# Second feature pair of the first chunk by seven block products, with its loads re-ordered, in a GeGLU kernel

## The chip, the cores and the metric

One NeuronCore of a Trainium2 chip. The metric is the device time of one execution in microseconds (us), shorter is better. Each kernel's runs were timed beside runs of the kernel before on the same chip. A **ratio** below is the mean time of one kernel's fast runs over the mean of the other's of the same rounds, so it is not quite the ratio of the medians that stand beside it; the square brackets hold its 95% interval.

## The reference, cut to what matters

```python
B, S, D, F = 1, 2048, 1024, 3584          # bf16 x [S, D], w_gate and w_up [D, F], w_down [F, D]
def reference(x, w_gate, w_up, w_down):
    return (gelu_tanh(x @ w_gate) * (x @ w_up)) @ w_down
```

## The kernel before

Tokens go in two halves of 1024, each two **token blocks** of 512. A **feature block** is 128 columns of the weights, a **pair** two of them, a **chunk** four (512 columns). D is eight slices of 128, called kd 0 to 7. A **slot** is one TensorE matmul of a 128x128 weight block with a 512 wide moving operand. One pair on two token blocks with both matrices is 2 x 2 x 2 x 8 = 64 slots when multiplied directly. From the second chunk on, every pair is done by Strassen's scheme in Winograd's form: seven products M1 to M7 of blocks of half of D instead of eight, 7 x 2 x 4 = 56 slots. M1 and M2 take the bf16 data as they lie; the five others take sums of weight blocks ("left sums", s1 to s4 and a22) and of x blocks ("right sums", t1 to t4 and b22) in the 32-bit type fp32r, which VectorE, GpSimd and ScalarE have to make first. A **bank** is one of the tiles that TensorE writes its results to. The very first chunk of the kernel is done directly, because there is nobody yet to have made sums. Its start:

```python
    load_x0(0, sp)                              # first 256 columns of x, token block 0
    load_w(first, 0, 0, 2, act, 0, FA)          # gate, kd 0-1, first 256 of 512 columns
    load_w(first, 1, 0, 2, sp, 0, FA)           # up
    load_x0(1, act)
    load_w(first, 0, 2, 5, act, 0, FA)
    load_w(first, 1, 2, 5, sp, 0, FA)
    # ... act table, identity, NWARM = 8 matmuls on constants ...
    for kd in range(KH, KD):                    # KH = 4, KD = 8
        load_xT(xT, 0, 0, kd, kd + 1)           # transposing loads of x, SyncE's queue
        if kd == KH + 1:
            for j in range(2):
                load_w(first, j, 5, KD, act, 0, FA)
    for j in range(2):
        load_w(first, j, 0, KD, sp, FA, FG)     # the other 256 columns, all kd
    for k0 in range(0, KD, KH):
        load_xT(xT, 0, 1, k0, k0 + KH)          # token block 1
    new_chunk((0, 1))
    for j in range(2):
        load_w((0, 1), j, 0, KD)
```

and its computation, ahead of the loop over the pairs:

```python
    def first_units(hT):                        # feature blocks 0 and 1, token block 0
        transpose_x0(0)                         # first x by TensorE transposes
        for kd, j in [(kd, j) for kd in range(KD) for j in range(2)]:
            for u in range(2):
                mm_gu(banks[held[u][j]], (wg, wu)[j], u, 0, kd)
            if (j, kd) == (1, 0):
                transpose_x0(1)
        # ...
            first_units(hT)
            unit(hT, PB, 2, 0)                  # unit(bank set, feature block, token block)
            t_sum("t1")
            unit(hT, QB, 3, 0)
            t_sum("t2")
            t_sum("b22")
            unit(hT, VB, 0, 1)
            t_sum("t3")
            for name in S_NAMES:                # left sums of the next chunk's first pair
                for j in range(2):
                    s_sum(0, PPG, j, name)      # on GpSimd
            unit(hT, RB, 1, 1)
            t_sum("t4")
            unit(hT, QB, 2, 1)
            unit(hT, VB, 3, 1)
```

## Time and profile before

| | before |
|---|---|
| time, median of 4 runs | 541.57 us (541.2 to 542.12) |
| instructions | 7102, of them 2392 matmuls and transposes |
| first pair of the second chunk starts at | 33.80 us |
| next pair after it | 12.56 us later |
| granted TensorE clock | full in every slice |

Two rows say what the first chunk is. The first line below is the page's header; the second is a group (line, engine, operation, shapes, count; then busy us and mean ns of one; then TensorE's idle time just ahead of them). The last two are the stretch 17 to 20 us in the windows view (busy us and number of instructions of TensorE, its weight loads, VectorE, ScalarE, GpSimd; granted clock; DMA share; GB/s).

```profile
span 539.7 us, 7102 instructions
```
```profile
L252 PE MATMUL bank<-xT,w_mem 128*128 128x512 bf16 x128 | 28.4, 379 | 0.3 <-DVE xT L310 0.2
```
```profile
core 0: us, PE busy (x) PEld busy (x) DVE busy (x) ACT busy (x) POOL busy (x), PEclk, DMA share, GB/s
...
17.00:20.00 3.00, 3.00 (x16) 1.35 (x15) 2.69 (x2) 1.54 (x4) 0.00 (x0) 1.00 1.07 291
```

The reader is to see that 128 direct slots stand in 28.4 us with 0.3 us of idle time ahead of all of them. There is nothing to win here but slots; the mark to watch is the start of the next chunk's first pair, 33.80 us, since everything behind it is the same program in both kernels.

### The profile page before, as it was taken

The numbers are of one execution on the slowest core, as the hardware profiler recorded it, in microseconds if no ns is written. First come the engines' busy times: TensorE is split into PE (matmuls) and PEld (weight loads), VectorE is DVE, ScalarE is ACT, GpSimd is POOL, SyncE is SP. The second block draws the span as 40 slices with busy tenths as digits, with TensorE's granted clock in tenths as the row PEclk, the third lists the DMA queues.
The fourth block names the chain that finished last, engine by engine and source line by source line (L and its number), as shares of the span: only waits on it lengthen the run. The fifth ranks groups of instructions, "written<-read, shape, count | busy, mean of one in ns | idle before, by whom it ended". The sixth has DMA issues, their size and how long they took to land.

```text
span 539.7 us, 7102 instructions
## 1 busy us (share of the span) xinstructions
PE 535.1 (99%) x2392; PEld 374.5 (69%) x2392; DVE 354.9 (66%) x466; ACT 258.9 (48%) x438; POOL 235.0 (44%) x206
## 2 busy tenths in 40 slices
PE   9999999999999999999999999999999999999997
PEld 3457777666776676767776677777777766866865
DVE  1767777787775997889574434444444469969951
ACT  2435555555555319216465555555555551452270
POOL 0197777777776000000056776666777730000000
PEclk9999999999999999999999999999999999999999
DMA  9928577696827876779950405041331466677946
GB/s 233 310 82 230 185 242 237 184 286 195 277 76 252 299 244 227 249 265 313 327 182 1 155 2 156 7 149 57 99 106 51 157 204 213 226 241 246 291 145 207
DMA packets 84771, 102.70 MB, mean 190 GB/s; under 512 B 18688, under 2 KB 66304, under 8 KB 84736
## 3 DMA queue, kind: packets, MB, share of 16 engines
q1 hardware_dynamic: 61936, 80.30, 46.2%
q10 hardware_dynamic: 22800, 21.96, 13.2%
q8 instruction: 19, 0.31, 0.2%
q14 instruction: 16, 0.13, 0.1%
HBM read 85.98 MB, written 12.58 MB: 183 GB/s over the span
## 4 chain that ended last, share of the span: by engine, by line
PE 98%; DMA 1%; ACTq 0%; ACT 0%; issue 0%
PE bank L386 61%; PE bank L656 33%; PE bank L252 5%; DMA w_mem<-in_w_gate_dram 1%; ACTq L161 0%; ACT xT L312 0%; ACT o_sb L709 0%; ACTq L167 0%; ACTq L709 0%
## 5 line engine op out<-in xcount | busy, mean ns | idle before, releaser
L386 PE MATMUL bank<-t_mem,s_mem 128*128 128x512 f32 x1016 | 239.8, 394 | 0.0
L386 PEld LDWEIGHTS bank<-t_mem,s_mem 128*128 128x128 f32 x1016 | 190.8, 188 | 41.9
L358 POOL TENSOR_TENSOR s_mem<-w_mem 128x512 fp32r<-128x512 bf16 x100 | 115.8, 1178 | 201.3 <-DMA w_mem<-in_w_up_dram 104.6
L276 DVE TENSOR_TENSOR hT<-w_mem,bank 128x512 bf16<-128x512 f32 x104 | 71.3, 686 | 92.4 <-PE bank L386 46.3
L656 PE MATMUL bank<-t_mem,s_mem 128*128 128x512 f32 x544 | 127.2, 392 | 0.0
L656 PEld LDWEIGHTS bank<-t_mem,s_mem 128*128 128x128 f32 x544 | 102.1, 188 | 22.2 <-issue 0.2
L409 DVE TENSOR_TENSOR bank<-bank,m 128x512 f32<-128x512 f32 x104 | 67.3, 694 | 46.9 <-ACT m L431 45.3
L386 PE MATMUL bank<-xT,w_mem 128*128 128x512 bf16 x416 | 94.3, 380 | 0.0
L271 ACT ACTIVATE w_mem<-bank 128x512 f32<-128x512 f32 x104 | 61.9, 596 | 57.7 <-DVE bank L409 32.7
L386 PEld LDWEIGHTS <-w_mem 128*128 128x128 bf16 x416 | 38.7, 98 | 49.7 <-issue 6.5
L566 DVE TENSOR_TENSOR t_mem<-w_mem 128x1024 fp32r<-128x1024 bf16 x56 | 65.5, 1216 | 0.0
L358 POOL TENSOR_TENSOR s_mem<-w_mem,s_mem 128x512 fp32r<-128x512 bf16 x50 | 62.1, 1267 | 0.0
L358 POOL TENSOR_TENSOR s_mem<-s_mem,w_mem 128x512 fp32r<-128x512 f32 x50 | 59.6, 1212 | 0.0
L371 ACT CAST s_mem<-w_mem 128x512 fp32r<-128x512 bf16 x52 | 32.0, 616 | 33.1 <-PE bank L386 29.1
L436 ACT COPY bank<-bank 128x512 f32<-128x512 f32 x52 | 29.6, 570 | 38.1 <-PE bank L386 38.1
L631 DVE TENSOR_TENSOR s_mem<-hT 128x512 fp32r<-128x512 bf16 x52 | 34.2, 685 | 10.2 <-PE bank L656 9.5
L656 PEld LDWEIGHTS <-hT 128*128 128x128 bf16 x224 | 21.3, 98 | 26.6 <-issue 2.1
L431 ACT COPY m<-bank 128x512 f32<-128x512 f32 x52 | 30.5, 587 | 17.1 <-PE bank L386 17.1
L440 ACT COPY bank<-bank 128x512 f32<-128x512 f32 x52 | 29.6, 570 | 13.5 <-PE bank L386 13.5
L709 ACT CAST o_sb<-bank 128x512 bf16<-128x512 f32 x28 | 15.4, 585 | 39.6 <-PE bank L656 39.6
L591 DVE TENSOR_TENSOR o_sb<-wd_sb,o_sb 128x512 fp32r<-128x512 bf16 x28 | 29.4, 1051 | 0.5
L252 PE MATMUL bank<-xT,w_mem 128*128 128x512 bf16 x128 | 28.4, 379 | 0.3 <-DVE xT L310 0.2
(42 smaller groups left out, 250.4 us busy)
## 6 DMA issues: line engine op xcount, KB each, us to landing
t_mem<-t_dram SPq DMA_DIRECT2D x56, 512.0 KB, 5.3
w_mem<-in_w_gate_dram ACTq DMA_DIRECT2D x10, 1024.0 KB, 5.6
w_mem<-in_w_up_dram ACTq DMA_DIRECT2D x10, 1024.0 KB, 9.1
wd_sb<-in_w_down_dram SPq DMA_DIRECT2D x28, 256.0 KB, 5.0
t_dram<-o_sb SPq DMA_DIRECT2D x28, 256.0 KB, 2.4
wd_sb<-in_w_down_dram SPq DMA_DIRECT2D x12, 512.0 KB, 8.8
w_mem<-in_w_down_dram SPq DMA_DIRECT2D x10, 512.0 KB, 6.1
w_mem<-in_w_down_dram SPq DMA_DIRECT2D x4, 1024.0 KB, 6.3
```

Of the source, the lines that this page charges most:

```text
L252: nc.tensor.matmul(ps[:], lhsT=w_sb[:, kd, fi * P : (fi + 1) * P], rhs=xT[tb][:, kd, :], start=(kd == 0), stop=(kd == KD - 1),)
L271: act(nc.scalar.activation(out=g_sb, in_=ps[:], func=ACT.Gelu_apprx_tanh))
L276: nc.vector.tensor_tensor(out=hT[:, fc, tb * TB : (tb + 1) * TB], in0=g_sb, in1=ps[:], op=ALU.mult,)
L358: pool(nc.gpsimd.tensor_tensor(out=t, in0=in0, in1=in1, op=op))
L371: act(nc.scalar.copy(out=t, in_=a(1, 1)))
L386: nc.tensor.matmul(banks[bank][:], lhsT=lhs[:, c, :], rhs=rhs[:, c, :], start=start and c == 0, stop=c == KH - 1, skip_group_check=True,)
L409: nc.vector.tensor_tensor(out=banks[dst][:], in0=banks[src][:], in1=m5[j][:], op=ALU.add)
L431: act(nc.scalar.copy(out=m5[j][:], in_=banks[V_[j]][:]))
L436: act(nc.scalar.copy(out=banks[RB[j]][:], in_=banks[QB[j]][:]))
L566: dve(nc.vector.tensor_tensor(out=t, in0=in0, in1=in1, op=ALU.subtract))
L631: dve(nc.vector.tensor_tensor(out=t, in0=in0, in1=in1, op=op))
L656: nc.tensor.matmul(banks[bset[u]][:], lhsT=lhs(i, u), rhs=rhs(i), start=start and i == 0, stop=stop and i == NS - 1, skip_group_check=True,)
```

## The change

The second pair of the first chunk (feature blocks 2 and 3) is done by the seven products as well: 56 slots for 64. Its M1 and M2 are put between the parts of the first pair; all its sums are made on VectorE; M3 goes ahead of M7, so that ScalarE has time for a copy; and the loads are sorted by when the new order of slots wants them, weights on ScalarE's queue, x on SyncE's (but for one 128 KB load each way at the head). The core of the diff:

```diff
-    NWARM = 8
+    NWARM = 7
@@ loads
-    load_x0(0, sp)
-    load_w(first, 0, 0, 2, act, 0, FA)
-    load_w(first, 1, 0, 2, sp, 0, FA)
-    load_x0(1, act)
-    load_w(first, 0, 2, 5, act, 0, FA)
-    load_w(first, 1, 2, 5, sp, 0, FA)
+    load_x0(0, sp, 0, 2)                       # now two halves by tokens
+    load_x0(0, act, 2, 4)
+    load_w(first, 0, 0, 2, sp, 0, FA)
+    load_w(first, 1, 0, 2, act, 0, FA)
+    load_x0(1, sp)
+    for j in range(2):
+        load_w(first, j, 2, KH, act, 0, FA)
+    load_w(first, 0, 0, KH, act, FA, FG)
     act(nc.scalar.preload_act_table(ACT.Gelu_apprx_tanh))
+    load_w(first, 1, 0, KH, act, FA, FG)
+    for j in range(2):
+        load_w(first, j, KH, KH + 2, act)
+    for kd in range(KH, KH + 2):
+        load_xT(xT, 0, 0, kd, kd + 1)
+    for j in range(2):
+        load_w(first, j, KH + 2, KD, act)
+    for kd in range(KH + 2, KD):
+        load_xT(xT, 0, 0, kd, kd + 1)
+    for kd in range(0, KD, 2):
+        load_xT(xT, 0, 1, kd, kd + 2)
     # (the old loads behind the warm-ups are gone)
@@ the first chunk, new
+        transpose_x0(0)
+        warm(PB[1])
+        first_pair_part(0, 0, 2)               # feature blocks 0, 1; token block 0; kd 0-1
+        transpose_x0(1)
+        first_pair_part(0, 2, KH)
+        on_x0(0, True)                         # M1
+        for j in range(2):
+            act(nc.scalar.copy(out=banks[QB[j]][:], in_=banks[VB[j]][:]))
+            sums(j, "s3")
+        first_pair_part(0, KH, KD)
+        sums(0, "s1", "s2", "s4")
         # ... activations; loads of the next chunk on ScalarE's queue ...
+        on_x0(1, False)                        # M2
+        sums(1, "s1", "s2", "s4")
+        t_sum("t1")
         # ...
+        first_pair_part(1, 0, KD)              # feature blocks 0, 1; token block 1
         # ... t2, b22, t3 in halves, activations ...
+        product(VB, "s1", "t1", True)          # M5
         # ... copies; GpSimd: s1 of the next pair ...
+        product(QB, "s2", "t2")                # M6
+        t_sum("t4", 0, KH // 2)
         # ... copies; GpSimd: s2 of the next pair ...
+        product(QB, "s4", "b22")               # M3
+        add_m5(QB[0], QB[0], 0)
+        t_sum("t4", KH // 2, KH)
+        product(RB, "s3", "t3")                # M7
+        add_m5(VB[0], RB[0], 0)
+        add_m5(QB[1], QB[1], 1)
+        add_m5(VB[1], RB[1], 1)
         # ... GpSimd: s3, s4 of the next pair; activations ...
+        product(RB, "a22", "t4")               # M4
```

## The prediction

> **What bounds the kernel now.** I read the chain of waits first, then the timeline of the first 36 us, then the groups and the traffic. The chain, in order of time:
>
> ```profile
> 1.82 5.65 DMA w_mem<-in_w_gate_dram
> 7.98 0.59 ACT xT L312
> 8.61 25.34 PE bank L252 x116
> 33.96 150.70 PE bank L386 x672
> ```
>
> From 8.6 us to the last store the chain lies on TensorE alone, so time can only be had in two ways: fewer matmul slots, or an earlier and smoother start. Two slot lengths come out of these rows: 25.34 / 116 = 0.218 us for the direct units of the first chunk (all bf16), 150.70 / 672 = 0.224 us for a Strassen pair (16 bf16 and 40 fp32r slots in 56, 12.56 us). If the bf16 slots stay at 0.218, an fp32r slot is (12.56 - 16 x 0.218) / 40 = 0.227 us. The first chunk is four feature blocks, two token blocks and two matrices, all by direct products, 128 slots. Its beginning, from the timeline:
>
> ```profile
> 0.77 3.43 PE L202 MATMUL bank<-const-bfloat16-1.0 128*128 128x512 bf16 x8 [0.77 <-PEq L961]
> 4.38 0.62 PE L302 MATMUL bank<-ident,w_mem 128*128 128x128 bf16 x8 [0.18 <-DMA w_mem<-in_x_dram]
> 5.24 1.02 PE L252 MATMUL bank<-xT,w_mem 128*128 128x512 bf16 x4 [0.24 <-DVE xT L310]
> 2.29 5.12 SPq L172 DMA_TRANSPOSE xT<-in_x_dram  x4
> 27.76 3.10 DVE L244 TENSOR_TENSOR t_mem<-xT,t_mem 128x2048 fp32r<-128x2048 bf16 x1
> 33.80 1.89 PE L386 MATMUL bank<-xT,w_mem 128*128 128x512 bf16 x8
> ```
>
> TensorE warms up on constants until 4.2, transposes the first x at 4.38, and reaches the first Strassen pair at 33.80. From 4.38 on that is 29.4 us for 128 slots (28.0) and 16 transposes (about 1.2), so only some 0.2 us are lost behind the first transpose. Three transposing loads out of four each hold SyncE about 1.25 us. That the first part is nevertheless fed is narrow, as the traffic by stretches says:
>
> ```profile
> core 0: us, PE busy (x) PEld busy (x) DVE busy (x) ACT busy (x) POOL busy (x), PEclk, DMA share, GB/s
> 2.00:5.00 3.00, 2.82 (x14) 1.09 (x13) 0.30 (x2) 1.28 (x1) 0.00 (x0) 1.00 1.01 283
> 5.00:8.00 3.00, 2.76 (x20) 1.37 (x19) 0.95 (x3) 0.02 (x1) 0.00 (x0) 1.00 1.29 250
> 8.00:11.00 3.00, 2.95 (x14) 1.14 (x13) 0.00 (x0) 0.56 (x1) 0.00 (x0) 1.00 1.17 262
> 11.00:14.00 3.00, 3.00 (x15) 1.35 (x15) 0.74 (x2) 1.08 (x2) 0.00 (x0) 1.00 1.25 287
> ```
>
> The DMA engines are full from 2 us on: cumulated 0.85 MB at 5, 1.60 at 8, 2.39 at 11, 3.25 at 14. VectorE, on the other hand, is nearly idle until 17 us.
>
> **What the Trainium skill says.** "TensorE: Matmul & The Clock Gate", Part 1, gives 215.7 ns from start to start for a warm 512-column matmul and a cold period of about 3.4 us; the 0.218 us slots and the eight warm-ups of 3.43 / 8 = 0.43 us agree. "DMA: Bandwidth & Descriptors", section "Issuing engines are not separate DMA queues", says that loads from several engines run on the same 16 DMA engines and interleave; the full DMA row above fits, so a second queue changes order and issue time, not the sum of the rates. "SBUF — State Buffer", section "SBUF: two separate sides", says that a VectorE operation with two SBUF inputs and a reading GpSimd operation exclude one another; the trace agrees that they cost each other time: L244 took 3.10 us beside GpSimd, against 2.28 for the same size in L236 alone.
>
> **The change, part by part.**
>
> *Slots.* The second pair costs 64 direct slots now, 64 x 0.218 = 13.98 us. After: 16 bf16 and 40 fp32r slots, 12.56 us. Gain **1.42 us**, if TensorE never waits.
>
> *Front.* The first x is cut into two halves, at the head of both queues. Before, the 128 KB of gate weights at the head of ScalarE's queue landed 3.4 us after issue at 0.73, thus at 4.13; the whole x (256 KB, one queue) released TensorE at 4.38. I expect the transposes at about 4.15: gain **0.2 us**, and one warm-up fewer fits that. The small wait for the copy (0.24) is now filled with a warm-up; I count nothing for it. Without any later wait the first chunk would then end at 33.8 - 1.6 = 32.15 us.
>
> *Loads by demand.* Here is the cost. Before, the first 64 slots need x of the first token block (1 MB) and half of the weights' columns (1 MB): 2 MB. After, M1 stands between the parts of the first pair, and the weights of the upper half of D come in full width; when TensorE wants up-weights of kd 6 it needs 3 MB (3.15 million bytes). Ahead of them stand 34 slots: 24 of the first pair (kd 0 to 5), 8 of M1 and 2 of the gate for kd 6. Without waits that is 4.15 + 1.2 (16 transposes) + about 0.5 (copies, the warm-up between) + 34 x 0.218 = 13.2. When do they land? By volume: 3.15 MB plus some 0.3 MB of the second token block that SyncE issues meanwhile, from the cumulated traffic at 14.5 us; but 1 MB of it now travels in 1024-byte pieces. The stretch 19 to 22 us, which holds such pieces only, ran at 370 GB/s, against 294 for 512-byte ones (11.3 to 12.8): that saves 0.7 us, 13.8. By issue: each queue entry behind the first eight waits for an earlier one on its semaphore. Transposing loads at 1.25 us each end their issue at about 7.9 (they wait for x, 4.1, then follow one another), the last lands about 2.4 us later, 10.3, as it did in the trace (7.4 to 9.8). The gate weights of kd 6 and 7 wait for exactly that one; the up weights follow at 10.8 and take the 3.4 us that such a load took before: 14.2. I take **14.0 us**. From there TensorE still has 6 slots of the first pair, 8 of M2, 32 of the second token block (46 x 0.218 = 10.03) and 40 fp32r (9.08), 19.1 us: end at **33.1 us**. The wait is thus about 0.8 us, in two or three pieces, since the lower half of the same weights (kd 4 and 5) comes just ahead.
>
> *VectorE.* It now makes the eight left sums of the pair (0.60 to 0.69 us each, rows of 128x512), four right sums (2.2 each), six products and four additions. From the landing of the kd 6 and 7 gate weights (13.5) I queue them in the order of the program: three sums to 15.6; two products after the activations to 17.0; three sums to 19.0; t1 to 21.2; M1+M2's product; t2, half of t3 to 24.9; products and the other half to 27.2; half of t4 to 28.5; addition to 29.5; other half to 30.9 (stretched by GpSimd as L244 was); addition that frees bank 6 at 31.5; two more to 32.8. M4's first half could start at 31.3, its second at 32.2. So TensorE waits about 0.2 for the first and 0.3 for the second, **0.5 us** in all. M5, M6, M3 find their sums ready by 1 to 2 us; M3 ahead of M7 gives ScalarE's copies the time they need (0.57 each, two in 1.8 us).
>
> *Sum.* The first Strassen pair of the next chunk starts at 33.1 + 0.5 = 33.6 instead of 33.8. Everything behind is the same program: 541.5 - 0.2 = **541.3 us**.
>
> **The rivals.** (a) *Clean gain.* The loads come 0.8 us earlier than I think (two queues full, larger pieces) and VectorE keeps ahead: first chunk ends at 32.2, time 539.9. For it: the loads are sorted by use, and the sums cut into halves look like the work of someone who watched these waits; against it: the full DMA row. (b) *Loads bind.* Waiting behind T loads on semaphores puts kd 6 at 15.5: TensorE waits 2.5 us, VectorE's row of sums starts later too, M4 waits 0.6; end at 35.2, time 542.9. For it: SyncE's 5.12 us for four transposing loads; against it: 1024-byte pieces share the engines well. (c) *VectorE or clock.* t4 and the additions of M7 become the bound (M4 waits 1.5 us), or with seven warm-ups a cold window remains and doubles a few slots: 542.3. Against it: the eight transposes ran in 0.62 us, already warm, before any long work. (d) The next chunk's loads, now from ScalarE's queue behind activations, could reach GpSimd late; its sums have 10 us until needed, so I give it nothing.
>
> **Range and chances.** The clean end is 539.9, the bad end 542.9; the three runs of before spread over 0.9 us. I say **541.3**, range **539.7 to 542.8**, the clean gain just inside and the loads that bind just outside, because the sorted loads make me hold (a) for a little likelier than (b). 2% would be 10.8 us; no rival reaches a third of it: faster 0.01, same 0.98, slower 0.01.
>
> **What would show it.** TensorE's instructions fall by 8, from 2392 to 2384; the transposes start near 4.15. Right if TensorE's idle time between 9 and 15 us, with gate or up weights as releaser, is near 0.8 us, and the first matmul of the pair after lies near 33.6. VectorE should release M4's first matmuls. Wrong if no wait on weights shows (a), or over 2 us (b), or if M5, M6 or M7 wait on sums, or if the later pairs are no longer evenly spaced at 12.56 us.

## The result, and the profile after

The changed kernel takes **546.87 us** (median of 4 runs, 545.35 to 547.42); the ratio to the kernel before is 1.0087 [1.0068, 1.0105]. That is within 2%, as predicted, but 5.3 us slower, outside the range, and on the other side of the kernel before. The page of the profiled execution (header, then TensorE's row of the clock):

```profile
span 545.6 us, 7086 instructions
...
PEclk9899999999999999999999999999999999999999
```

The span is 5.9 us longer. The chain of waits (start us, length, what) shows where, and that the later pairs are evenly spaced at 12.56 us as before, so that all of the loss lies ahead of 39.7 us:

```profile
1.75 5.29 DMA w_mem<-in_x_dram
7.06 4.18 DMA w_mem<-in_w_up_dram
11.26 6.56 DMA w_mem<-in_w_up_dram
17.87 2.34 PE bank L253 x6
20.21 2.54 PE bank L365 x8
...
34.44 0.70 DVE bank L395
35.14 1.70 DVE t_mem L248
36.84 0.62 DVE bank L395
```

Before, the chain left the transfers at 7.5 us and lay on TensorE from 8.6 on. Now two loads of up weights in a row, from 7.06 to 17.8 us, set TensorE's pace; then VectorE does, at 34.4 to 37.5. The waits view of TensorE for 9 to 19 us (engine, line, releaser: us in all, times, longest) adds up what the weights cost, 2.2 + 0.8 + 0.5 = 3.5 us:

```profile
PE bank L253 <- DMA w_mem<-in_w_up_dram: 2.2, 2, 1.7
...
PE bank L253 <- DMA w_mem<-in_w_gate_dram: 0.8, 2, 0.5
PE bank L365 <- DMA w_mem<-in_w_up_dram: 0.5, 1, 0.5
```

The timeline (start, length, engine, line, operation, count; in brackets the idle time before it and what ended it) has the marks that answer to those of before:

```profile
2.25 12.92 SPq L172 DMA_TRANSPOSE xT<-in_x_dram  x8
...
3.71 0.63 PE L297 MATMUL bank<-ident,w_mem 128*128 128x128 bf16 x4
...
17.87 2.34 PE L253 MATMUL bank<-xT,w_mem 128*128 128x512 bf16 x6 [1.69 <-DMA w_mem<-in_w_up_dram]
...
20.00 2.75 PE L365 MATMUL bank<-xT,w_mem 128*128 128x512 bf16 x8
...
22.59 7.07 PE L253 MATMUL bank<-xT,w_mem 128*128 128x512 bf16 x31
...
37.51 2.39 PE L365 MATMUL bank<-t_mem,s_mem 128*128 128x512 f32 x8 [0.40 <-DVE bank L395]
...
39.74 1.90 PE L365 MATMUL bank<-xT,w_mem 128*128 128x512 bf16 x7
```

The transposes start 0.67 us earlier than before (3.71 against 4.38), as hoped for and more. But the last up weights (kd 6 and 7) release TensorE only at 17.87; M2 (20.00) and token block 1 (22.59) follow; M4 (37.51) waits for VectorE; the first pair of the next chunk starts at 39.74, 5.94 us later than before. Between 17.87 and 22.59 stand 14 slots; at 0.218 us each they are 3.05 us, they took 4.72. The windows view says why (columns as above, the clock is the third number from the end):

```profile
14.00:17.00 3.00, 1.79 (x8) 0.45 (x6) 1.39 (x2) 0.00 (x0) 0.00 (x0) 1.00 1.20 250
17.00:20.00 3.00, 2.13 (x6) 0.80 (x7) 0.81 (x2) 1.03 (x2) 0.00 (x0) 0.72 1.13 341
20.00:23.00 3.00, 3.00 (x11) 1.21 (x10) 2.93 (x5) 1.13 (x4) 0.00 (x0) 0.71 1.01 321
```

TensorE was granted half its clock for 3.41 us, from 18.31 to 21.72 (0.28 x 3 + 0.29 x 3 = 1.7 us of clock lost). In the 3.41 us just before (14.90 to 18.31, same view) it had been busy for 1.33 us.

Last, the DMA view from the start to the landing of those weights (queue: packets, MB, share of 16 engines; q10 is ScalarE's queue, which has now carried all 2.10 MB that it was given for this part, 1.97 MB of weights and half of the first x; q1 is SyncE's):

```profile
q1 hardware_dynamic: 7272, 2.06, 58.0%
q10 hardware_dynamic: 3232, 2.10, 46.8%
```

SyncE's queue had moved 2.06 MB by then. Of these TensorE wanted 1.05 MB; the other 1.0 MB is nearly the whole of token block 1 (1.05 MB), whose transposing loads SyncE issued without a pause until 15.2 us (first timeline line).

### The profile page after: what moved, and what is told of

Read it like the earlier page. It is cut to its first block, busy times and chain, and to the rows that moved or that the text cites. A ratio compares the mean times of both kernels' runs of the same rounds, so it can differ in the third digit from the quotient of the medians.

```text
span 545.6 us, 7086 instructions
## 1 busy us (share of the span) xinstructions
PE 535.1 (98%) x2348; PEld 377.6 (69%) x2384; DVE 363.5 (67%) x482; ACT 262.8 (48%) x445; POOL 235.0 (43%) x206
## 4 chain that ended last, share of the span: by engine, by line
PE 95%; DMA 3%; DVE 1%; issue 0%; SPq 0%; ACT 0%; ACTq 0%; DVEq 0%
PE bank L365 61%; PE bank L734 32%; DMA w_mem<-in_w_up_dram 2%; PE bank L253 2%; DMA w_mem<-in_x_dram 1%; DVE t_mem L248 0%; DVE bank L395 0%; ACT o_sb L787 0%; SPq L161 0%; SPq L167 0%; ACTq L787 0%; DVEq L395 0%
## 5 line engine op out<-in xcount | busy, mean ns | idle before, releaser
L365 PE MATMUL bank<-t_mem,s_mem 128*128 128x512 f32 x1056 | 250.0, 395 | 0.4 <-DVE bank L395 0.4
L365 PEld LDWEIGHTS bank<-t_mem,s_mem 128*128 128x128 f32 x1056 | 198.1, 188 | 44.9 <-DVE bank L395 1.3
L734 PE MATMUL bank<-t_mem,s_mem 128*128 128x512 f32 x544 | 127.2, 393 | 0.0
L734 PEld LDWEIGHTS bank<-t_mem,s_mem 128*128 128x128 f32 x544 | 102.1, 188 | 22.3 <-issue 0.2
L365 PE MATMUL bank<-xT,w_mem 128*128 128x512 bf16 x406 | 97.8, 382 | 1.9 <-DMA w_mem<-in_w_up_dram 0.5
L365 PEld LDWEIGHTS <-w_mem 128*128 128x128 bf16 x432 | 40.4, 99 | 53.4 <-issue 8.2
L357 ACT CAST s_mem<-w_mem 128x512 fp32r<-128x512 bf16 x54 | 33.1, 615 | 30.5 <-PE bank L365 29.2
L509 ACT COPY m<-bank 128x512 f32<-128x512 f32 x52 | 30.7, 589 | 17.1 <-PE bank L365 17.1
L641 ACT CAST t_mem<-w_mem 128x1024 fp32r<-128x1024 bf16 x28 | 26.9, 1047 | 0.0
```

The source lines that it names most:

```text
L357: act(nc.scalar.copy(out=t, in_=a(1, 1)))
L365: nc.tensor.matmul(banks[bank][:], lhsT=lhs[:, c, :], rhs=rhs[:, c, :], start=start and c == 0, stop=c == KH - 1, skip_group_check=True,)
L509: act(nc.scalar.copy(out=m5[j][:], in_=banks[V_[j]][:]))
L734: nc.tensor.matmul(banks[bset[u]][:], lhsT=lhs(i, u), rhs=rhs(i), start=start and i == 0, stop=stop and i == NS - 1, skip_group_check=True,)
```

## The experiments

Theory T: the transposing loads of token block 1 run beside the weights and take their bandwidth, which makes the last up weights late (3.9 us); the gaps then cost a stretch of half clock (1.7 us), and VectorE's row of sums adds the rest. Rivals: the order of issue and its semaphores alone make the weights late (I); the seven products with their sums on VectorE are what costs, however the loads lie (S). The table has the marks of each profiled execution.

| kernel | token block 1 starts | next chunk's pair starts | median us | ratio to before |
|---|---|---|---|---|
| before | (other order) | 33.80 | 541.57 | 1 |
| the change | 22.59 | 39.74 | 546.87 | 1.0087 |
| a2_again | 22.01 | 39.44 | 548.01 | 1.0094 [1.0066, 1.0121] |
| e1_hold_x1 | 17.70 | 43.63 | 552.29 | 1.0178 [1.0144, 1.0212] |
| e7_lanes_only | 23.18 | 40.33 | 548.40 | 1.0114 [1.0076, 1.0152] |
| e8_merged | 21.62 | 39.06 | 547.98 | 1.0105 [1.0075, 1.0135] |
| e2_fill | 22.16 | 39.82 | 549.32 | 1.0125 [1.0089, 1.0162] |
| e3_up_on_pool | 21.03 | 38.20 | 546.95 | 1.0082 [1.0049, 1.0114] |
| e3b_pool_behind | 20.45 | 37.06 | 547.72 | 1.0100 [1.0074, 1.0125] |
| e5_seven_alone | 17.02 | 36.09 | 546.93 | 1.0087 [1.0061, 1.0114] |
| b2_both | 17.61 | 34.18 | 542.60 | 1.0013 [0.9981, 1.0045] |
| b3_fed_seven | 18.83 | 35.20 | 543.09 | 1.0017 [0.9996, 1.0037] |
| b4_fed_split | 17.48 | 34.15 | 542.03 | 0.9997 [0.9977, 1.0017] |
| b5_old_front (wrong result) | 16.52 | 33.45 | 543.21 | 1.0015 [0.9998, 1.0032] |
| b6_x_halves (wrong result) | 19.24 | 35.61 | 544.27 | 1.0041 [1.0019, 1.0064] |
| b7_repaired | 18.09 | 34.43 | 541.41 | 0.9974 [0.9950, 0.9997] |

The median and the start of the pair do not always move together. In some executions a stretch at 115 to 137 us costs another 2 to 3.5 us (1.2 in e1, 5.4 in e8, where a half clock stretch at 138 us is added); it is told under a2_again. Therefore the starts are what I compare for the first chunk, and the times only with that in mind. Each start is one execution; the changed kernel itself was profiled twice, 0.3 us apart.

### The loads

**e1_hold_x1**: the changed kernel, but the loads of token block 1 wait until the last up weights have landed.

```diff
     for j in range(2):
-        load_w(first, j, KH + 2, KD, act)
+        last_w = load_w(first, j, KH + 2, KD, act)
@@
     for kd in range(0, KD, 2):
-        load_xT(xT, 0, 1, kd, kd + 2)
+        t = load_xT(xT, 0, 1, kd, kd + 2)
+        if kd == 0:
+            tc.add_manual_dep(t.ins, last_w.ins.name, SYNC_DEP, reason="hold")
```

> The changed kernel; only the transposing loads of the second token block (1 MB) are held until the last up weights of the first chunk have landed. Theory T (these loads take about half of the DMA engines from 8 to 17 us, so the last weights land at 17.9 instead of my 14.0): the last weights land at 14 to 14.8, TensorE's waits on weights between 9 and 18 us fall from 3.6 to about 1 us, no cold-clock window, first pair of the next chunk near 34, time 541 to 542.5. Rival I (the weights are issued too late, each behind an earlier load's semaphore): last weights land at 16.5 or later, time 545 or more.

Measured, the chain of waits of this kernel, and its DMA view from the start to 14.1 us:

```profile
9.00 5.10 DMA w_mem<-in_w_up_dram
...
18.11 10.61 DMA xT<-in_x_dram
```
```profile
q10 hardware_dynamic: 3232, 2.10, 54.8%
q1 hardware_dynamic: 3248, 1.05, 39.4%
```

The same 2.10 MB have now landed at 14.10 us instead of 17.8, with 1.05 MB beside them instead of 2.06. The engines were no less busy in the change: its DMA view to 14.0 us has 3.18 MB, but only 1.61 of them on q10. TensorE waits only 0.2 us for weights between 9 and 19 us, and the clock stays full there; token block 1 could start at 17.70. So it is shown that the loads of token block 1 make the weights late. Two things are in these 3.7 us: the last up weights are issued at 9.00 instead of 11.26, and land after 5.10 us instead of 6.56. Behind the first eight, a load is issued when an earlier one has landed, and in e1 that is another one: gate weights issued at 3.48, in the change up weights issued at 7.06. How much of the earlier issue comes from emptier engines and how much from this, e1 does not say. As a cure it failed: the held loads start at 14.1, meet the next chunk's 2 MB of weights and 1 MB of down weights, and the last lands at 28.7. TensorE waits 1.36 and 3.83 us for them, loses clock, and the pair starts at 43.63. The time was missed for that reason. Token block 1 has no slack to give away.

**e7_lanes_only**: the same edit, but the hold is on an early load (gate, kd 0 to 3, second columns), meant to change the assignment of semaphores as in e1 while token block 1 is hardly held.

```diff
-    load_w(first, 0, 0, KH, act, FA, FG)
+    last_w = load_w(first, 0, 0, KH, act, FA, FG)
```

> As the run before, but held only until the gate weights of the lower half have landed (about 8.8 us, when these loads are issued anyway): the hold is without effect, while the assignment of semaphores to loads changes in the same manner as there. Theory T: last weights land at 16.5 to 18, time within 1.5 us of the changed kernel (545 to 547.5). Rival I: the changed assignment alone brings the weights by 2 us or more, time below 544.

The last up weights release TensorE at 18.46, after a wait of 2.60 us; the pair starts at 40.33. This is as late as in the changed kernel. But the run is no clean control, as the traces show: its last up weights waited for the landing of the up weights issued at 7.20, as in the change (7.06), and not for gate weights as in e1; and the first load of token block 1 was held until 9.82, against 7.42. So it does not show that the assignment of semaphores did nothing in e1.

**e8_merged**: kd 4 to 7 of each matrix in one load of 512 KB, issued 0.6 us earlier (10.70 instead of 11.26 for the last).

```diff
     for j in range(2):
-        load_w(first, j, KH, KH + 2, act)
+        load_w(first, j, KH, KD, act)
@@
-    for j in range(2):
-        load_w(first, j, KH + 2, KD, act)
```

> The changed kernel with the upper half's weights as one 512 KB load for each matrix instead of two of 256 KB: they are issued by about 9.5 us instead of 11.3. Rival I: last weights land by 15.5, time 543 or less. Theory T: the engines are shared all the same, last weights land at 16.5 or later; kd 4 now waits for the larger load; time 545 to 547.

The up weights release TensorE for the last time at 16.86, one microsecond earlier; the pair starts at 39.06, 0.7 us earlier. So 0.6 us of earlier issue gave at most 1 us of 3.9, and perhaps nothing: in e2, with the loads of the change, the last up weights land at 17.1, in a2 at 18.4, here at 16.8. How much issue alone would bring if it came 2.3 us earlier, as in e1, no run shows by itself; what speaks against rival I as the main cause is that the engines are full in the change. Moreover, this execution kept its clock here and the change lost 1.7 us to it, so of the 0.7 us at the pair nothing can be put down to the merged loads.

**e5_seven_alone**: the seven products with all loads exactly as before and the first pair in one piece; M1 and M2 follow it.

```diff
-    (all loads of the change)
+    (all loads of the kernel before; NWARM = 8)
@@
-        first_pair_part(0, 2, KH)
+        first_pair_part(0, 2, KD)
+        for u in range(2):
+            unit_out(hT, FIRST[u], u, 0)
         on_x0(0, True)
@@
-        first_pair_part(0, KH, KD)
```

> The seven products with all loads as in the kernel before: the first pair whole on the first token block, then M1 and M2 of the second pair. Theory T: no wait on weights over 1 us and no cold window; 8 slots fewer (1.4 us). But VectorE starts its sums only at 14.4 us, when the second columns' up weights land, so M4 waits 1 to 2 us: time 541 to 543, first pair of the next chunk at 33.5 to 35. If the loss of the changed kernel comes from the seven products themselves (their sums), this one is as slow: 545 or more.

```profile
17.02 7.07 PE L254 MATMUL bank<-xT,w_mem 128*128 128x512 bf16 x31
...
33.28 3.02 PE L366 MATMUL bank<-t_mem,s_mem 128*128 128x512 f32 x8 [1.80 <-DVE bank L396]
```

In the timeline token block 1 starts at 17.02, 5.6 us earlier than in the change: with the old loads, weights cost no more than one wait of 0.6 us. But now TensorE is so early that M4 waits 1.80 us for VectorE, and a half clock stretch follows (all four runs have a mean clock of 0.996); the pair starts at 36.09. The hoped-for time near that of before was missed. So S is right on one point: once the loads are mended, the sums bind. They were in part hidden behind the late weights in the change, where M4 waited 0.40 us by the timeline.

### The sums and the clock

**e2_fill**: 19 matmuls of zeros in front of the four waits for weights of kd 4 to 7, so that TensorE is never idle there.

```diff
+    FILL = {(KH, 0): 4, (KH, 1): 3, (KH + 2, 0): 4, (KH + 2, 1): 8}
@@
             for j in range(2):
+                if tb == 0:
+                    fill(FIRST[0][0], FILL.get((kd, j), 0))
```

> The changed kernel with 19 matmuls of a zero matrix added to a bank in accumulation (they add nothing), 4, 3, 4 and 8 of them ahead of the four waits on the upper half's weights. Theory C (the wait of 1.7 us and those before it let the clock fall to half for 3.4 us, which costs 1.7 us): no half-clock window, first pair of the next chunk 1.2 to 1.7 us earlier than in the changed kernel (39.7), near 38.2, time near 545. Rival: the clock window costs nothing of itself because the last weights' landing and VectorE's row of sums set the end; first pair at 39 or later.

The clock stayed full in all four runs (0.999 to 1.0), as theory C has it; alone this is weak, since e3 below kept it in all four as well, with its gaps unfilled. The profiles say more: behind the warm-ups and ahead of 40 us, each half clock stretch follows 3.41 us in which TensorE was busy for 24 to 47% (39% in the change, 35% in a2, 24% in e7, 34% in e1, 44% in b6, 47% in e5), and with the fillers it was busy for 98% or more from 12 to 22 us. Nothing was won: the fillers ran until 19.14, though the last up weights had landed at 17.1, and the pair starts at 39.82. The size of the clock's share is not settled by this run. It is by e3, which has the same loads and kept its clock: from the release by the last up weights to token block 1 it needs 3.03 us (18.00 to 21.03), the change 4.72. The runs of the change agree roughly. Of its eight (four in the first round, four in a2_again), four have a mean clock of 0.996 or 0.997 and four of 0.999 or 1.0; 3.41 us at half clock are 0.3% of the span. The means of the two groups are 548.3 and 546.5 us, near half of 3.41 us; but one run of the first group (550.68) has a second loss, told under a2_again, and without it the difference is 1.0. The clock costs some 1.7 us, in half of the executions, and the kernel is slower than before without it.

**e3_up_on_pool**: the left sums of the up matrix on GpSimd, which is idle then.

```diff
-                s_sum(0, pair, j, name, True, False)
+                s_sum(0, pair, j, name, j == 0, False)
```

> The changed kernel with the four left sums of the up matrix on GpSimd, idle at that time, instead of VectorE. If M4's waits (0.8 and 0.3 us) come from the length of VectorE's row, taking 2.4 us from it removes them: first pair of the next chunk at 38.6 to 39.2 instead of 39.7. Rival: the two engines exclude one another on their shared port, VectorE's sums grow by what is taken away, first pair at 39.5 or later.

M4 still waits 0.45 us in the timeline, and the halves of t4 take 1.60 and 1.81 us. Taking four sums off VectorE hardly helps, since the additions of the end wait for t4, and t4 is slow. The pair starts at 38.20, mostly because this execution kept its clock.

**e3b_pool_behind**: GpSimd's first sums for the next pair wait until VectorE has made t4.

```diff
         product(QB, "s2", "t2")
         t_sum("t4", 0, KH // 2)
@@
         t_sum("t4", KH // 2, KH)
+        pool_behind_dve()
+        for name in ("s1", "s2"):
+            for j in range(2):
+                s_sum(0, nxt, j, name)          # (taken out further up)
```

> The changed kernel with GpSimd's sums for the next pair held until VectorE has made the second half of t4. If it is GpSimd that stretches the sums (1.59 and 1.79 us for halves that take 1.15 undisturbed), these fall to 1.2 and M4's waits fall from 1.1 to 0.2 us or less: first pair at 38.7 to 39.0; the next pair then waits up to 0.5 us for its own sums. Rival: M4 waits as before, first pair at 39.7.

```profile
27.17 10.05 PE L365 MATMUL bank<-t_mem,s_mem 128*128 128x512 f32 x40
...
30.70 1.22 DVE L248 TENSOR_TENSOR t_mem<-xT,t_mem 128x1024 fp32r<-128x1024 bf16 x1
...
32.92 1.22 DVE L248 TENSOR_TENSOR t_mem<-xT,t_mem 128x1024 fp32r<-128x1024 bf16 x1
```

The two halves of t4 take 1.22 us each, against 1.59 and 1.79 in the change, and all 40 fp32r slots stand in one row of the timeline: M4 waits no more. From the start of M5 to the next pair it is now 9.89 us, against 10.43 in the change, so 0.5 us of the loss is GpSimd beside VectorE. The weights still come late (17.42 us), and the profiled execution lost some 2.7 us behind the pair, in the stretch at 115 us.

### All at once

**b2_both**: the loads of before (second columns in four pieces), the first pair in one piece, GpSimd behind t4.

```diff
     (e5, and)
-    for j in range(2):
-        load_w(first, j, 0, KD, sp, FA, FG)
+    for k0 in range(0, KD, KH):
+        for j in range(2):
+            load_w(first, j, k0, k0 + KH, sp, FA, FG)
     (and e3b; the gate's left sums ahead of the first activations)
```

> Loads as in the kernel before, except that the second columns come in four pieces (gate and up of the lower half, then of the upper half); first pair whole, then M1 and M2; the gate's left sums ahead of the first products on VectorE; GpSimd's sums behind t4. From the run with the seven products alone (M7 ends at 31.3, M4 then waits 1.8 us and a half-clock window follows): VectorE is 2 to 3 us earlier, so that M4 waits 0.3 us at most, no half-clock window, first pair at 32.5 to 33.2 against 33.8 before, time 540.3 to 541.5. If the seven products can't be fed here at all, M4 waits 1 us or more, and the time is over 542.5.

The pair starts at 34.18, 5.6 us earlier than in the change, without a wait for VectorE; the time is 542.60 and equal to before. Loads (with the order of slots that goes with them), VectorE's order with GpSimd behind it, and the clock together account for the whole loss; this run changes them at once and does not part them.

**a2_again**: the changed kernel once more.

> The changed kernel again, unaltered, on the chip of this call, so that the runs beside it can be compared with it: 545.3 to 548; last up weights at 17 to 18.5 us, M4 waits about 1 us. Open: whether the profiles of the variants, in six of eight of which a stretch at 117 to 137 us (the transposing loads of the second half's x beside a 2 MB weight chunk) lost some 3 us of its own, differ from the changed kernel there. If that stretch is hit here too, it is the chip's traffic and not the variants.

The pair starts at 39.44, again with a half clock stretch, and 0.71 us of waiting for VectorE at M4. The order differs: the longest wait for weights, 1.84 us, is that for kd 4 and 5, which release TensorE at 15.64; the half clock lies from 15.52 to 18.93, and the last up weights land at 18.4. So 39.7 was no accident. This execution ended late, at 548.9 us; its chain of waits shows a second loss, which the first profile of the change hasn't:

```profile
119.44 10.22 DMA o_sb<-in_x_dram
129.68 1.99 DMA x_dram<-o_sb
```

Two transposing loads for the second half of the tokens run beside the next chunk's 2 MB of weights here and land after 10.2 us. VectorE's staging buffers then come free late, and TensorE loses the time. The same stretch is in the profiles of e1, e2, e3, e3b, e7, e8, b3 and b5 (8.5 to 10.2 us for the slower of the two loads), not in those of before, the change, e5, b2, b4, b6 and b7, where it lands in 7.5 to 8.2 us. As the unaltered kernel shows both, it belongs to the execution. Some runs of the kernel before are at 543 to 544.5 us while most are at 541.7; that this is the same stretch is argued, since none of them was profiled.

**b3_fed_seven** and **b4_fed_split**: e5's loads, and b2's, with the second half of t4 ahead of the additions, and the addition that frees M4's bank first.

```diff
         product(QB, "s4", "b22")
-        add_m5(QB[0], QB[0], 0)
         t_sum("t4", KH // 2, KH)
+        (GpSimd's s1, s2 behind it)
+        add_m5(QB[0], QB[0], 0)
         product(RB, "s3", "t3")
         add_m5(VB[0], RB[0], 0)
-        add_m5(QB[1], QB[1], 1)
         add_m5(VB[1], RB[1], 1)
+        add_m5(QB[1], QB[1], 1)
```

> The loads exactly as in the kernel before, first pair whole, then the seven products; the gate's left sums first on VectorE, GpSimd's sums behind t4, the second half of t4 ahead of the additions, and the addition that frees M4's second bank ahead of the other. From the run with the seven products alone (M2 ends at 17.0) and the last one (no wait from there on: 16.5 us to the next pair): first pair at 33.2 to 33.6 against 33.8 before, time 541.0 to 541.5, ratio 0.9985 to 1.0000. If 8 fewer slots were worth 1.4 us here, the first pair would come at 32.4 and the time be 540.2.

> As the run before, with the second columns' weights in four pieces: M1 of the up matrix need not wait for the whole column (0.5 us), but the smaller loads may come in the way of the first columns' last up weights (which cost 0.5 us in the run that had them): first pair at 32.8 to 34.0, time 540.6 to 541.8.

In b3 the first x came late (transposes at 5.09) and TensorE waited 1.20 us for up weights; the pair starts at 35.20. In b4 it starts at 34.15, with no wait for weights and 0.24 us at M4; the time equals that of before. In b4 the first matmul follows 1.6 us after the first transpose (6.08 against 4.49), where the kernel before needs 0.86 (5.24 against 4.38): the new order of the transposes, in two banks with a filler between, costs 0.7 us at the front.

**b5_old_front**: b4 with before's order of the first slots, without the filler, and the transposes through four banks.

```diff
-            tp = banks[VB[(q + n) % 2]][:].bitcast(BF16)
+            tp = banks[(VB + QB)[(3 * q + n) % 4]][:].bitcast(BF16)
@@
-        warm(PB[1])
-        first_pair_part(0, 0, 2)
+        first_pair_part(0, 0, 1)
         transpose_x0(1)
```

> As the last run with the second columns in four pieces, but x's transposes on four banks and in the order of the kernel before (first matmuls after kd 0 and 1, the others' transposes behind kd 0), without the filler matmul. If the front ate the gain: first matmul within 0.9 us of the first transpose, first pair at 33.0 to 33.4, time 540.7 to 541.2, ratio 0.997 to 0.999. Rival: the first columns' weights land when they land (about 11 us), and the front's time is made up there: first pair at 33.9 or later, ratio 1.000.

**b6_x_halves**: b5 with the first x in two halves on two queues, as in the change, and seven warm-ups.

```diff
-    load_x0(0, sp)
+    load_x0(0, sp, 0, 2)
+    load_x0(0, act, 2, 4)
```

> As b5, with the first x in two halves at the head of both queues and seven warm-ups, as in the changed kernel: transposes at 3.7 to 4.2 instead of 4.4 to 4.5. If the loads behind are not moved, 0.3 us more are gained: first pair at 32.7 to 33.2. Rival: the weights behind come later by as much, nothing is gained.

Both gave a wrong result (relative error 0.185), which was not intended. The transposes now went through the QB banks, onto which ScalarE later copies M1, for M6 to add to. "PSUM — Partial Sum Buffer", section "The four PSUM rules", of the Trainium skill states that writes by ScalarE and VectorE leave the bits alone that tell a matmul whether to add or to overwrite, that a transpose clears the bank's bits, and that a bf16 transpose was not seen to set them on its output. So M6 would have overwritten M1. The runs agree: b7, which moves the transposes to banks that a starting matmul takes next, is right. As the work is the same, the starts may still be read: 33.45 in b5, 0.35 earlier than before, and 35.61 in b6. In b6 the transposes begin at 3.71, but then TensorE waits 0.71 us for gate weights and 1.19 for the next part of x: the earlier start of the change gains nothing, the wait moves behind it. On top comes a half clock stretch from 7.83 to 11.25, after 3.41 us with 1.50 busy; it costs some 1.5 of the 2.2 us between b5 and b6 (28 slots from 8.27 on take 7.52 us, in b5 6.04).

**b7_repaired**: b5 with the transposes in banks 2, 3 and 1, and one left sum of the up matrix made earlier.

```diff
-            tp = banks[(VB + QB)[(3 * q + n) % 4]][:].bitcast(BF16)
+            tp = banks[(VB + PB[1:])[n]][:].bitcast(BF16)
```

> b5 repaired: x's transposes on banks 2, 3 and 1, correct result expected; VectorE 0.6 us earlier. First matmul about 1 us after the first transpose, M4 waits 0.1 us at most, first pair at 32.8 to 33.3 against 33.8, time in runs not struck by the stretch at 117 to 137 us 540.6 to 541.1; ratio over all runs 0.997 to 1.001, since that stretch struck about half of the runs of every variant. Rival: first pair at 33.8 or later, nothing gained.

```profile
12.46 2.33 PE L255 MATMUL bank<-xT,w_mem 128*128 128x512 bf16 x9 [1.38 <-DMA w_mem<-in_w_up_dram]
...
24.80 9.79 PE L367 MATMUL bank<-t_mem,s_mem 128*128 128x512 f32 x40
...
34.43 1.90 PE L367 MATMUL bank<-xT,w_mem 128*128 128x512 bf16 x7
```

The result is right, and the median of six runs is 541.41 us, against 541.78 beside it; ratio 0.9974 [0.9950, 0.9997]. The ratio flatters it, as four of the eleven runs of before are at 543.9 to 544.5; by the medians it is 0.4 us. The profiled execution was the slowest of the six (542.7) and had a wait of 1.38 us for weights, so the pair starts at 34.43; the 40 fp32r slots take 9.63 us without a wait for VectorE that the timeline shows. This is the best version of the seven products, and worth less than a third of the 1.42 us that its eight slots promise.

## Why the prediction was wrong

The sign and the range were wrong; the class "within 2%" was right. By its own steps, with the starts from the timeline:

- **Slots: right.** The page counts 2384 weight loads on TensorE, eight fewer than before, as predicted (36 of the matmuls' own records are missing). The second chunk's pairs are spaced at 12.56 us.
- **Front: right in its first part, without worth.** The transposes came 0.2 us earlier still than the 4.15 predicted, but the second part of x landed only at 7.06. At 9.7 us the change has done 16 slots, the kernel before some 18; b6 shows the same exchange, with a half clock stretch on top.
- **Loads by demand: here it failed.** The step reads "3.15 MB plus some 0.3 MB of the second token block that SyncE issues meanwhile", and gives 14.0 us. In its place the whole 1.0 MB of token block 1 ran beside the weights, and the last of them came at 17.87: **+3.87 us**. The time for issue (10.8) was nearly right, 11.26 in the trace; what was wrong was to give a load 3.4 us to land, as before, when it took 6.6 beside a second queue full of transposing loads. Nor is the 0.7 us to be seen that 1024-byte pieces were to save: by 14.0 us the change had moved 3.18 MB in all, the kernel before 3.27. e1 shows the size of the error: with 3.15 MB only, the landing is at 14.10. That this meets the predicted 14.0 is in part luck: the load was issued at 9.00 and took 5.10 us, where 10.8 and 3.4 were predicted. (A slip of the sum besides: 3.45 MB are reached at 14.7 by the prediction's own table, not at 14.5.) Rival (b), "loads bind", had the right direction, and issue did wait for landings as it says, but with 15.5 us it was still 2.4 too early.
- **Clock: named as a rival for the warm-up, left out for the waits.** 14 slots took 4.72 us instead of 3.05, **+1.67 us** in the profiled execution, and in half of the change's eight runs. The prediction had 0.8 us of waiting and so no reason for it.
- **Token block 1 and the fp32r slots.** 32 slots took 6.72 us (22.59 to 29.31) instead of 6.98, and 40 fp32r slots take 9.63 in b7 instead of 9.08. Together **+0.29 us**: this is partly where one row ends and the next begins, and some 0.3 us of short waits are in b7's row, as the later pair needs 9.30 for its 40 (35.98 to 45.28).
- **VectorE: right in kind, too small.** From M5's start to the next pair it is 10.43 us, 0.80 more than b7's 9.63, where 0.5 was predicted: **+0.30 us**. t4's halves took 1.59 and 1.79 us beside GpSimd; only the second was counted as stretched, and at 1.4.

The sum is 3.87 + 1.67 + 0.29 + 0.30 = 6.13 us; predicted was 33.6, the trace has 39.74, 6.14 later. The eight slots are gone, but they were off the path: the last weights, not the number of slots, set the end of the first part.

What stays open: why the seven products don't gain their full 1.42 us in b7. In its one profile the pair starts 2.05 us later than 33.80 - 1.42 = 32.38: some 0.4 us are the later first x (transposes at 4.79 against 4.38), 1.38 the wait for up weights, 0.3 the fp32r row. No other execution of it was seen from inside. Open is also how the earlier landing in e1 divides between issue and emptier engines.

## What to carry to other kernels

When a change moves loads, count every byte that any queue will have in flight until the load you need has landed, not only the bytes that stand ahead of it in its own queue: a queue that is free to issue takes its share, and sorting each queue by use orders nothing between the queues. Fewer matmul slots in a part that lives from its transfers are worth nothing until the transfers are counted again, and a wait of some microseconds can cost a stretch of half clock on top. When one bound is removed (e5), look at once for the one that was hidden behind it.

## What the Trainium skill lacked or had wrong

- "DMA: Bandwidth & Descriptors", section "Issuing engines are not separate DMA queues", says that queues interleave, and the traces agree (from 8 to 17.9 us the two queues of the change moved 1.34 and 1.32 MB); it gives no figure for how the time to land grows. Here a 256 KB weight load took 6.6 us from issue to landing beside SyncE's transposing loads (11.26 to 17.8; the two queues had moved 2.06 and 2.10 MB), 5.1 us with those held back (e1), and a 192 KB load of up weights 3.4 us in the kernel before.
- "TensorE: Matmul & The Clock Gate", Part 1, puts the loss of the clock after an idle window of about 3.4 us. Here no single gap of the change was longer than 1.7 us, and the clock fell after 3.41 us with 1.33 busy. No page gives the busy share at which it falls. In this case's profiles it fell after stretches that were busy for 24 to 47%, and held in e8 and e3 after stretches of 42% (1.43 and 1.44 us of 3.41, at 11.71 and 12.23) and in e3b of 57%: the limit lies somewhere near 45%, and these figures do not part it sharply. Since the stretches of 3.41 us begin at another point in each execution, the same waits can cost the clock in one and not in the next, which would fit the change's eight runs, four of each kind. The length of 3.41 us agrees.
- "SBUF — State Buffer", section "SBUF: two separate sides", names the exclusion of VectorE and GpSimd but no size: a VectorE difference of 128x1024 took 1.22 us alone and 1.59 to 1.81 beside GpSimd, and 1.22 again when GpSimd was held (e3b).
